# Fused key turning, fences on the carried part, and a new instruction order in a retention-plus-channel-mix kernel

## The chip, the cores and the metric

The kernel runs on one core of a Trainium2 chip, as one program. The metric is the device time of one execution in microseconds. TensorE (PE) multiplies, VectorE (DVE) and ScalarE (ACT) move and combine, GpSimd (POOL) and SyncE (SP) issue most of the transfers.

## The reference

Two layers follow each other. Batch 4, 8 heads, 768 tokens, head size 64; model size 512, inner size 1024.

```python
state = gamma * state + einsum('bhd,bhe->bhde', k[:, :, t], v[:, :, t])
y[:, :, t] = einsum('bhd,bhde->bhe', q[:, :, t], state) / sqrt(D)
...
x_prev = x shifted by one token
xk = mu_k * x + (1 - mu_k) * x_prev
xr = mu_r * x + (1 - mu_r) * x_prev
out = sigmoid(xr @ w_r) * (relu(xk @ w_k) ** 2 @ w_v)
```

Here x is y with the heads side by side.

## The kernel before

The work is cut into 12 blocks of 256 tokens, three to each batch entry, so blocks 0, 3, 6 and 9 begin a sequence. A block passes through retention and then through the channel mix.

Retention of block n, by the short names that the kernel gives its steps: `lq`, `lk`, `lv` load queries, keys and values (GpSimd's queue mostly). `vs` scales the values by the decay. `Tq` and `Tk` turn queries and keys on PE, `Eq` and `Ek` copy the turned blocks from PSUM on ACT. `S` multiplies turned keys by turned queries (scores, in two parts for blocks 0 to 5), and `M` masks them on DVE. `C` makes the products of keys and values that change the state; `U` adds them up (DVE, two sums in blocks 0 to 5 and four in the later ones); `G` decays the sum for the next block (ACT). The output is gathered in one pair of PSUM banks: `I` adds the part of the carried state whose input rows and output bank lie crosswise, `Y` the part inside the block, and `J` the rest of the carried part (in blocks 0, 1 and 6 to 11 `Y` includes it). `D` multiplies by the decay table `gy` on DVE and gives x.

Channel mix: `dx` is the difference of neighbouring tokens, `X.n.0.j` and `X.n.1.j` are the mixed inputs for w_k and w_r, four pieces each (DVE; for block 0 `t` prepares them on ACT). `K` multiplies by w_k, `Qa` and `Qb` take Relu and square on ACT, `R` and `s` make the gate, `V` multiplies by w_v, `O` combines on DVE, `st` stores. Blocks 3 and 4, 6 and 7, 9 and 10 share their mixed inputs and `K` in pairs.

Three sets of blocks differ in the tiles used. Blocks in `WHOLE` are turned with 128-row tiles: 16 matmuls of 128 rows and 64 columns. The others are turned in quarters of the array: 32 matmuls of 64 by 64. `HALF` (6 to 11) also does its scores, products and outputs in quarters of the array. `WIDE` (2 to 5) uses whole 128-row products.

The order of everything is written out by hand in the string `ORDER`: each word is one step, `~` names its engine and `@` the PSUM banks of a PE step. The loop at the end of the kernel calls the steps in that order, and each engine executes its own in that order. Waits between engines follow from the data. `z` steps multiply zeros, to keep PE busy while it would wait at the start.

Of the kernel before, what the change touches and what calls it, by code (L numbers as in the profile page):

```python
# [9 lines left out]
F16 = mybir.dt.float16  # L10
# [18 lines left out]
wk.1~p G.0~a z.2@6 Tq.1@6 Eq.1~a vs.1~p lq.2~p Tk.1@7 Ek.1~a M.0.0.0.2~v M.0.1.2.4~v Y.0 D.0~v
t.0.0.3~a t.0.0.2~a t.0.0.1~a lv.2~p z.2@4 S.1.1@23 M.1.1~v C.1@01 U.1.0~v z.2@4 I.1@23 S.1.0@67  # L30
X.0.0.1~v t.0.1.2~a X.0.0.2~v Tk.2@0 t.0.1.3~a t.0.0.0~a M.1.0~v X.0.0.0~v z.2@4 Y.1 t.0.1.1~a
X.0.0.3~v Ek.2~a K.0.0@0 K.0.1@6 lq.4~p U.1.1~v G.1~a wr~p lk.4~p D.1~v dx.1~v X.1.0.2~v X.1.0.0~v
K.0.2@1 Qa.0.0~a Qb.0.0~a Qa.0.2~a lq.3~p X.1.0.1~v X.1.0.3~v X.1.1.0~v Qa.0.1~a K.0.3@0 Qa.0.3~a
lk.3~p vs.2~v Tq.2@1 X.1.1.2~v K.1.3@6 K.1.0@0 C.2@7 U.2.0~v lv.3~p Eq.2~a S.2.1@23 M.2.1~v S.2.0@45
M.2.0~v Qb.0.3~a lv.4~p K.1.1@1 X.1.1.1~v Qa.1.0~a t.0.1.0~a K.1.2@7 I.2@23 Qb.0.1~a Qa.1.1~a wv.0~p
Qb.0.2~a Tq.4@01 Eq.4~a Y.2 Qa.1.3~a Qb.1.1~a X.0.1.3~v X.1.1.3~v R.1.1@4 Tk.4@01 Ek.4~a J.2 R.1.0@6
Qa.1.2~a s.1.0~a X.0.1.2~v X.0.1.1~v X.0.1.0~v R.0.1@5 s.0.1~a s.1.1~a R.0.0@7 s.0.0~a S.4.1@01
Qb.1.0~a D.2~v dx.2~v X.2.0.2~v X.2.0.0~v S.4.0@23 Tq.3@4 Eq.3~a X.2.0.1~v wv.1~p X.2.0.3~v Tk.3@7
lq.5~p Ek.3~a K.2.2@5 Qa.2.2~a K.2.3@4 M.4.1~v M.4.0~v Qa.2.3~a Qb.2.3~a lk.6~p S.3.1@67 M.3.1~v
S.3.0@01 vs.3~p C.3@23 U.3.0~a Qb.2.2~a K.2.1@4 Qa.2.1~a K.2.0@2 Qa.2.0~a I.3@45 lq.6~p vs.4~v  # L40
C.4@67 U.3.1~v X.2.1.1~v V.0.1.0@3 M.3.0~v V.1.0.0@2 G.3~a U.4.0~v I.4@01 X.2.1.3~v U.4.1~v J.3
Qb.1.3~a Y.4 Qb.2.0~a lk.5~p X.2.1.2~v X.2.1.0~v Y.3 D.3~v dx.3~v V.0.0.0@7 V.0.1.1 O.0.1~v Tq.5@45
J.4 D.4~v dx.4~v R.2.0@6 Qb.2.1~a V.0.0.1 O.0.0~v X.3.0.1~v Eq.5~a Qb.1.2~a V.1.0.1 X.3.0.2~v
O.1.0~v Tq.6@01 Eq.6~a Tk.6@45 Ek.6~a st.0.0~s lk.7~p st.1.0~s V.1.1.0@3 V.1.1.1 O.1.1~v s.2.0~a
R.2.1@0 s.2.1~a lv.5~p X.3.0.0~v X.3.0.3~v Tk.7@67 Ek.7~a G.4~a S.6@45 M.6~v Tk.5@23 Ek.5~a vs.5~v
V.2.0.0@0 K.3.2@1 Qa.3.2~a K.3.0@6 S.5.0@23 M.5.0~v S.5.1@45 C.5@1 U.5.0~v K.3.3@7 Qb.3.2~a Qa.3.0~a
lq.7~p K.3.7@6 Qa.3.3~a Qa.3.7~a lv.6~p lq.8~p vs.6~v M.5.1~v V.2.0.1 st.0.1~s I.5@67 O.2.0~v
st.2.0~s C.6@23 U.6.0~a U.6.1~v U.6.2~v K.3.6@1 Qa.3.6~a lk.9~p X.3.1.3~v Y.5 Tq.7@45 Eq.7~a U.6.3~v
X.3.1.2~v I.6@01 J.5 X.3.1.0~v D.5~v X.3.1.1~v Qb.3.3~a G.6~a V.2.1.0@2 K.3.1@3 V.2.1.1 O.2.1~v
Qb.3.7~a Qa.3.1~a Qb.3.1~a dx.5~v K.3.4@4 K.3.5@5 Qa.3.5~a X.5.0.0~v X.5.0.3~v R.3.1@2 s.3.1~a  # L50
lv.7~p Qa.3.4~a X.5.0.1~v Qb.3.4~a R.3.0@5 R.4.0@2 s.3.0~a s.4.0~a Qb.3.0~a X.5.0.2~v vs.7~v K.5.2@4
S.7@67 st.1.1~s M.7~v Qb.3.5~a Y.6 Qb.3.6~a lv.10~p C.7@23 U.7.0~v X.5.1.1~v Qa.5.2~a K.5.0@5
R.4.1@6 Qa.5.0~a D.6~v s.4.1~a V.4.0.0@4 V.4.0.1 V.3.1.0@5 U.7.1~v Qb.5.0~a X.5.1.3~v U.7.2~v I.7@01
X.5.1.2~v U.7.3~v Tq.8@67 Eq.8~a X.5.1.0~v O.4.0~v lv.8~p vs.8~v Qb.5.2~a lq.10~p lk.8~p Tk.8@23
Ek.8~a V.3.1.1 V.3.0.0@4 C.8@67 O.3.1~v st.2.1~s st.3.1~s Y.7 dx.6~v D.7~v Tq.10@23 V.3.0.1 Eq.10~a
G.7~a dx.7~v X.6.0.2~v V.4.1.0@5 R.5.1@2 s.5.1~a K.5.3@0 Qa.5.3~a R.5.0@2 U.8.0~v O.3.0~v V.4.1.1
lv.9~p lk.10~p lq.9~p Tk.10@01 s.5.0~a U.8.1~v X.6.0.1~v Ek.10~a X.6.0.0~v Tk.9@23 Ek.9~a K.5.1@7
Qa.5.1~a X.6.0.3~v K.6.0@4 lq.11~p Qb.5.1~a Qa.6.0~a U.8.2~v I.8@01 vs.9~v S.8@23 M.8~v O.4.1~v
# [26 lines left out]
def kernel(  # L85
# [126 lines left out]
    def first(n):  # L212
        return n % NB == 0
# [586 lines left out]
```

## Time and profile before

| | |
|---|---|
| times shown | 153.05, 240.62 (median), 286.7 us |
| span of the profiled execution | 151.4 us |
| around the span (153.05 less 151.4) | 1.65 us |
| granted TensorE clock | 1.00 |
| PE busy | 143.4 us, 95% |
| DVE busy | 127.8 us, 84% |
| ACT busy | 103.6 us, 68% |
| POOL busy | 55.3 us, 37% |
| transferred | 22.16 MB |

The profile is of one execution; its span belongs to the lowest of the three times. Busy time of an engine is the union of its instructions, so matmuls that overlap count once. An instruction's own duration contains its way through the pipeline; what a step costs in a dense stretch is the distance from its start to the next step's start.

### The profile page before, as it was taken

To read this page: it belongs to the slowest core of one execution; us is meant where nothing else is said; L and a number is where in the kernel's file an instruction comes from. 1 tells how busy PE (TensorE), PEld (TensorE's weight loads), DVE (VectorE), ACT (ScalarE), POOL (GpSimd) and SP (SyncE) were. 2 spreads that over 40 slices of the span, in tenths; PEclk is the share of its full clock that TensorE was granted. 3 is DMA by queue.
4 is the path that set the end of the run, shared out by engine and by line. 5 is a ranking of instruction groups with operands and counts; after the bars stand their busy time and mean duration, and the time that the engine had idled before them with its cause. 6 is when DMAs were issued, how large, how long until landed. Compare 5 with 4: busy or idle time off the path is not lost.

```text
span 151.4 us, 5541 instructions
## 1 busy us (share of the span) xinstructions
PE 143.4 (95%) x2426; PEld 82.8 (55%) x2426; DVE 127.8 (84%) x212; ACT 103.6 (68%) x195; POOL 55.3 (37%) x65
## 2 busy tenths in 40 slices
PE   7878799999999999999999999999999999999991
PEld 3345487757754554547465564548456444655450
DVE  7886999999989999999999999999799999400432
ACT  3565979899844795779567786999604756839420
POOL 7953998577957309996710000000000000000000
PEclk9999999999999999999999999999999999999999
DMA  5999999999999999999999019301000005500433
GB/s 140 219 229 197 207 231 192 168 251 212 196 167 202 233 262 107 256 300 198 231 173 126 7 38 283 105 35 45 0 4 0 4 0 211 205 0 0 148 133 139
DMA packets 45624, 22.16 MB, mean 146 GB/s; under 512 B 37400, under 2 KB 41248, under 8 KB 45600
## 3 DMA queue, kind: packets, MB, share of 16 engines
q0 software_dynamic: 38704, 14.42, 74.5%
q1 hardware_dynamic: 6592, 7.21, 14.3%
q8 instruction: 19, 0.31, 0.8%
q10 hardware_dynamic: 304, 0.18, 0.4%
q14 instruction: 5, 0.04, 0.1%
HBM read 24.16 MB, written 6.29 MB: 201 GB/s over the span
## 4 chain that ended last, share of the span: by engine, by line
PE 73%; DMA 12%; POOL 11%; issue 1%; DVE 0%; POOLq 0%
PE ps L624 27%; PE ps L572 14%; DMA v<-in_v_dram 12%; PE ps L612 12%; PE ps L582 8%; PE ps L278 3%; POOL q L235 3%; POOL k L230 2%; PE ps L441 2%; POOL vs L253 2%; POOL v L230 2%; PE ps L366 1%; PE ps L462 1%; PE ps L642 1%; PE ps L318 1%
## 5 line engine op out<-in xcount | busy, mean ns | idle before, releaser
L624 PE MATMUL ps<-wv,k2s 128*128 128x512 f16 x184 | 44.1, 380 | 0.0
L591 ACT ACTIVATE kr<-ps 128x512 f32<-128x512 f32 x48 | 27.9, 594 | 12.5 <-PE ps L582 6.5
L624 PEld LDWEIGHTS <-k2s 128*128 128x128 f16 x184 | 17.1, 98 | 18.9 <-ACT k2s L603 0.4
L630 DVE SCALAR_TENSOR_TENSOR os<-ps,rs 128x512 f32<-128x512 f32 x23 | 15.6, 684 | 11.9 <-ACT rs L618 9.4
L612 PE MATMUL ps<-wr,xr 128*128 128x512 f16 x96 | 23.5, 379 | 0.0
L582 PE MATMUL ps<-xk,wk 128*128 128x256 f16 x192 | 23.2, 273 | 0.0
L572 PE MATMUL ps<-xk,wk 128*128 128x512 f16 x96 | 23.0, 379 | 0.0
L618 ACT ACTIVATE rs<-ps 128x512 f32<-128x512 f32 x24 | 13.6, 597 | 12.9 <-PE ps L612 12.1
L230 POOL DMA_DIRECT2D k<-in_k_dram x20 | 17.8, 903 | 10.3 <-PE ps L384 6.7
L582 PEld LDWEIGHTS <-wk 128*128 128x128 f16 x192 | 18.1, 98 | 3.7
L241 ACT COPY qT<-ps 128x1024 f16<-128x1024 f16 (+1 forms) x13 | 12.3, 946 | 9.5 <-PE ps L278 7.8
L558 DVE SCALAR_TENSOR_TENSOR xr<-dx,mu,xT 128x256 f16<-128x256 f32 (+1 forms) x32 | 17.9, 577 | 0.1
L230 POOL DMA_DIRECT2D v<-in_v_dram x18 | 16.0, 911 | 3.6 <-DMA wr<-in_moe_w_r_dram 1.9
L558 DVE SCALAR_TENSOR_TENSOR xk<-dx,mu,xT 128x256 f16<-128x256 f32 (+1 forms) x32 | 17.0, 579 | 0.2
L354 DVE TENSOR_TENSOR a<-ps,c_sb 128x1024 f16<-128x1024 f32 (+1 forms) x14 | 14.6, 1066 | 0.9 <-PE ps L339 0.6
L603 ACT ACTIVATE k2s<-kr 128x512 f16<-128x512 f32 x24 | 14.8, 631 | 0.3
L612 PEld LDWEIGHTS <-xr 128*128 128x128 f16 x96 | 9.0, 97 | 10.7 <-issue 0.5
L572 PEld LDWEIGHTS <-wk 128*128 128x128 f16 x96 | 9.1, 98 | 10.5
L599 ACT ACTIVATE k2s<-kr 128x512 f16<-128x512 f32 x24 | 14.5, 627 | 0.3
L241 ACT COPY kT<-ps 128x1024 f16<-128x1024 f16 (+1 forms) x13 | 12.2, 945 | 2.2 <-PE ps L272 1.7
L529 DVE TENSOR_TENSOR dx<-xT 128x1024 f32<-128x1024 f32 x11 | 13.4, 1221 | 0.2
L253 DVE TENSOR_TENSOR vs<-v,csm_sb 128x1024 f16<-128x1024 f32 x10 | 12.2, 1217 | 0.2 <-DMA v<-in_v_dram 0.2
(73 smaller groups left out, 165.6 us busy)
## 6 DMA issues: line engine op xcount, KB each, us to landing
out_dram<-os SPq DMA_DIRECT2D x23, 256.0 KB, 2.4
v<-in_v_dram POOLq DMA_DIRECT2D x18, 256.0 KB, 7.7
q<-in_q_dram POOLq DMA_DIRECT2D x11, 256.0 KB, 8.4
k<-in_k_dram POOLq DMA_DIRECT2D x21, 128.0 KB, 8.8
v<-in_v_dram POOLq DMA_DIRECT2D x2, 512.0 KB, 7.2
wk<-in_moe_w_k_dram POOLq DMA_DIRECT2D x2, 512.0 KB, 10.4
wv<-in_moe_w_v_dram POOLq DMA_DIRECT2D x2, 512.0 KB, 10.4
wr<-in_moe_w_r_dram POOLq DMA_DIRECT2D x1, 512.0 KB, 8.7
```

The costliest lines, as they stand in the source:

```text
L230: e.dma_start(out=dst[:, :, i * D : i * D + D], in_=src[:, i * P : i * P + P].rearrange("h p d -> p h d"),)
L241: e.copy(out=out, in_=in_)
L253: e.tensor_tensor(out=VS(n), in0=V32(n).rearrange("p h (i d) -> p i h d", i=2), in1=gks[:, int(half(n) or wide(n)), :, :, None].to_broadca ...
L354: nc.vector.tensor_tensor(out=a_full(n)[:, i, :, j0:j1], in0=pairs(banks("S", n, i, j0))[:, :, j0:j1], in1=(below if wide(n) else causal[: ...
L558: nc.vector.scalar_tensor_tensor(out=XM[w](k)[:, j, t0:t1], in0=DX(k)[:, j, t0:t1], scalar=mu[:, w * NCO + j : w * NCO + j + 1], in1=x[:, ...
L572: nc.tensor.matmul(banks("K", n, g), lhsT=wk16[:, co, g * P : g * P + P], rhs=XM[0](k)[:, co, :], start=(co == 0), stop=(co == NCO - 1),)
L582: nc.tensor.matmul(pz[:, i, :], lhsT=wk16[:, co, fo * P : fo * P + P], rhs=XM[0](k)[:, co, m * TM + t0 : m * TM + t1], start=(i == 0 and c ...
L591: nc.scalar.activation(out=kr, in_=banks("K", n, g, *u), func=AF.Relu)
L603: nc.scalar.activation(out=K2(n)[:, w * g : w * g + w, t0:t1], in_=kr.rearrange("p a t -> p (a t)").rearrange("p (i t) -> p i t", i=w), fu ...
L612: nc.tensor.matmul(banks("R", n, tb), lhsT=XM[1](k)[:, co, t : t + P], rhs=wr16[:, co, :], start=(co == 0), stop=(co == NCO - 1),)
L624: nc.tensor.matmul(banks("V", n, tb), lhsT=K2(n)[:, fo, tb * P : tb * P + P], rhs=wv16[:, fo, :], start=(fo == 0), stop=(fo == NFO - 1),)
L630: nc.vector.scalar_tensor_tensor(out=OS(2 * n + tb), in0=banks("V", n, tb), scalar=1.0 / (KSC * KSC), in1=RS(2 * n + tb), op0=ALU.mult, op ...
```

## The change

Five things change.

1. Blocks 4 and 5 are added to `WHOLE`, so their queries and keys are turned by 16 matmuls of 128 rows.
2. In blocks 6 to 11 (`MERGED`) `Tk` and `C` fall away. A new step `TC` multiplies each block of K by two things side by side, a 64 by 64 identity and the scaled values, 128 columns in one pass. It has two parts, `TC.n.0` and `TC.n.1`, of 16 matmuls each. The identity stands ahead of the values in the same buffer, which therefore has a ninth group of 64 columns and is filled by three new small steps on DVE. `Ec` copies the turned part, now in 32-bit PSUM, in two halves of 512 on ACT in place of one copy of 1024.
3. A new step `w` stands behind each `I`: ACT copies a few elements of the bank pair into a small buffer. What is accumulated there next waits for that copy.
4. The weights w_k come in three parts (quarter, half, quarter) in place of two halves, and the values of block 11 move from SyncE's queue to GpSimd's. The scaling of block 3's values moves from GpSimd to DVE.
5. The string `ORDER` is another one.

```diff
-WHOLE = (0, 1, 2, 3)
+WHOLE = (0, 1, 2, 3, 4, 5)
 WIDE = (2, 3, 4, 5)
+MERGED = (6, 7, 8, 9, 10, 11)
...
-    VS = ring("vs_", 3, [2, H, D], F16)
+    VI = ring("vs_", 3, [2 * H + 1, D], F16)
...
+    def VS(n):
+        return VI(n)[:, 1:].rearrange("p (i h) d -> p i h d", i=2)
...
+    fenced = const.tile([P, 2, NJ, 2], F32, name="fenced")
...
+    def both(n, i):
+        return banks("TC", n, i).rearrange("p u (j x t) -> p u j x t", j=NJ, x=2)
+
+    def turned_state(e, n, i):
+        ps = both(n, i)
+        for j in range(NJ):
+            for u in range(2):
+                for a, h, jo, hp in heads(j):
+                    k = 1 + i * H + h
+                    x = slice(0, 2) if more(n) or not (u and i) else slice(0, 1)
+                    nc.tensor.matmul(
+                        ps[low(a), u, j, x], lhsT=K16(n)[low(u), h, i * D : i * D + D],
+                        rhs=VI(n)[low(u), 0 : k + 1 : k][:, x],
+                        start=(j == 0), stop=(j == NJ - 1), skip_group_check=True,
+                    )
+
+    def turned_k_part(e, n, i):
+        copy(
+            e, KT(n)[:, :, i].rearrange("c j (u p) -> c u j p", u=2), both(n, i)[:, :, :, 0],
+        )
...
+        if merged(n):
+            src = both(n, c // 2)[:, c % 2, :, 1]
...
+    def fence(e, n):
+        us = slice(0 if half(n) or not first(n) else 1, 2)
+        e.copy(out=fenced[:, us], in_=pairs(banks("I", n))[:, us, :, 0:C:W])
...
-            ((step, 2, ALU.is_ge), (below, 0, ALU.is_ge)),
+            ((step, 2, ALU.is_ge), (below, 0, ALU.is_ge))
+            + tuple((VI(i)[:, 0], 2, ALU.is_equal) for i in range(3) if MERGED),
...
-    def load_wk(e, h):
-        f = slice(h * dff // 2, (h + 1) * dff // 2)
+    def load_wk(e, a, b):
+        f = slice(a * dff // 4, b * dff // 4)
```

Of the new `ORDER`, one piece before and the piece that stands for it now:

```diff
-D.2~v dx.2~v X.2.0.2~v X.2.0.0~v S.4.0@23 Tq.3@4 Eq.3~a X.2.0.1~v wv.1~p X.2.0.3~v Tk.3@7
+D.2~v K.1.0@1 U.3.1~v dx.2~v S.4.1@67 Qa.1.0~a G.3~a S.3.0@45 M.3.0~v X.2.0.1~v Qb.1.0~a
```

The first place is DVE from the output of block 2 (`xT0<-ps`) on. In the names, `xk_2` is the mixed input for `K` of block 2, `a2` the masked scores, `vs` the scaled values, `t32` and `tg2` the state sums. Before:

```order
L514 TENSOR_TENSOR xT0_130<-ps_61,gy_sb_122 128x2x4x128
L529 TENSOR_TENSOR dx_0_99<-xT0_130 128x4x256
L558 SCALAR_TENSOR_TENSOR xk_2_103<-dx_0_99,mu_125,xT0_130 128x256 x4
L354 TENSOR_TENSOR a2_1_84<-ps_61,c16_sb_120 128x1024 x2
L354 TENSOR_TENSOR a2_0_83<-ps_61,c16_sb_120 128x1024
L253 TENSOR_TENSOR vs_1_75<-v32_0_70,csm_sb_121 128x1024
```

and with the change:

```order
L547 TENSOR_TENSOR xT0_130<-ps_61,gy_sb_122 128x2x4x128
L452 TENSOR_TENSOR t32_0_86<-ps_61,tg2_0_93 128x256
L566 TENSOR_TENSOR dx_0_99<-xT0_130 128x4x256
L364 TENSOR_TENSOR a2_0_83<-ps_61,c16_sb_120 128x1024
L595 SCALAR_TENSOR_TENSOR xk_2_103<-dx_0_99,mu_125,xT0_130 128x256
L364 TENSOR_TENSOR a2_0_83<-ps_61,c16_sb_120 128x1024
L263 TENSOR_TENSOR vs_1_75<-v32_0_70,csm_sb_121 128x1024
L364 TENSOR_TENSOR a2_1_84<-ps_61,c16_sb_120 128x1024
L452 TENSOR_TENSOR tg2_1_94<-ps_61,tg0_1_88 128x256
L595 SCALAR_TENSOR_TENSOR xk_2_103<-dx_0_99,mu_125,xT0_130 128x256 x2
L452 TENSOR_TENSOR t32_0_86<-ps_61,tg2_1_94 128x256
L595 SCALAR_TENSOR_TENSOR xk_2_103<-dx_0_99,mu_125,xT0_130 128x256
```

The masks of blocks 3 and 4, the scaling of block 4's values and the state sums, which stood behind the four mixed inputs of block 2, stand between them now.

The second place is ACT, where block 6 begins (`qT_77` and `kT_80` are its turned queries and keys). Before:

```order
L241 COPY qT_77<-ps 128x2x4x128
L241 COPY kT_80<-ps 128x2x8x64
L618 ACTIVATE rs_112<-ps 128x512
L618 ACTIVATE rs_113<-ps 128x512
L241 COPY kT_81<-ps 128x2x8x64
```

and with the change, where `fenced` is the new small copy:

```order
L251 CAST tg_0_90<-ps 128x256
L251 COPY qT_77<-ps 128x2x4x128
L555 COPY fenced<-ps 128x16
L251 CAST kT_80<-ps 128x2x4x64
L628 ACTIVATE kr_107<-ps 128x512
L628 ACTIVATE kr_110<-ps 128x512
L636 ACTIVATE k2s<-kr_107 128x2x256
L251 CAST kT_80<-ps 128x2x4x64
```

One copy of the turned keys has become two, with other work between them, and the fence of block 5 stands ahead of the first.

The third place is GpSimd's queue around the values of block 3 (`v_3_73`). Before:

```order
L738 DMA wr_129<-in_moe_w_r_dram 128x4x512
L230 DMA k_0_66<-in_k_dram 128x8x64 x2
L235 DMA q_3_65<-in_q_dram 128x8x128
L230 DMA k_3_69<-in_k_dram 128x8x64 x2
L230 DMA v_3_73<-in_v_dram 128x8x64 x2
```

and with the change:

```order
L245 DMA q_3_65<-in_q_dram 128x8x128
L245 DMA q_0_62<-in_q_dram 128x8x128
L240 DMA v_3_73<-in_v_dram 128x8x64 x2
L240 DMA k_3_69<-in_k_dram 128x8x64 x2
L773 DMA wk_127<-in_moe_w_k_dram 128x4x256
L776 DMA wr_129<-in_moe_w_r_dram 128x4x512
```

The values of block 3 are issued ahead of the keys of block 3 and of the gate weights w_r, and the last quarter of w_k comes behind them.

More of the change, by code (lines that the diff above doesn't have):

```diff
@@ L29 @@
[L29 to L34, printed above, removed]
@@ L81 @@
+Vc.11.1.0@2 Oc.11.1.0~v sc.11.1.0~s
 """
```

127 lines of the change are left out of this document (68 added, 59 removed).

## The prediction

> **What bounds the kernel now.** I read the page first, then the busy times by stretch, then the end of the chain that ended last, then the timeline around the first blocks.
>
> ```profile
> PE 143.4 (95%) x2426; PEld 82.8 (55%) x2426; DVE 127.8 (84%) x212; ACT 103.6 (68%) x195; POOL 55.3 (37%) x65
> ...
> PE   7878799999999999999999999999999999999991
> ...
> DVE  7886999999989999999999999999799999400432
> ...
> POOL 7953998577957309996710000000000000000000
> ```
>
> TensorE (PE) is at nine tenths or more from the sixth slice to the last but one; VectorE (DVE) is as full, but stops ten slices before the end.
>
> ```profile
> core 0: us, PE busy (x) PEld busy (x) DVE busy (x) ACT busy (x) POOL busy (x), PEclk, DMA share, GB/s
> 0.00:10.00 10.00, 7.77 (x90) 3.87 (x90) 8.29 (x31) 4.78 (x10) 8.62 (x14) 1.00 1.10 178
> 10.00:20.00 10.00, 7.76 (x230) 5.24 (x230) 8.11 (x14) 7.13 (x16) 6.34 (x7) 1.00 1.51 220
> 20.00:30.00 10.00, 9.92 (x160) 7.92 (x158) 9.82 (x16) 8.88 (x18) 7.72 (x9) 1.00 1.67 196
> 30.00:38.00 8.00, 7.67 (x140) 5.07 (x140) 7.93 (x12) 7.94 (x14) 6.26 (x8) 1.00 1.30 229
> 38.00:50.00 12.00, 12.00 (x230) 7.08 (x230) 11.51 (x16) 7.05 (x15) 9.16 (x11) 1.00 1.90 192
> 50.00:60.00 10.00, 10.00 (x197) 5.13 (x195) 9.81 (x13) 8.07 (x15) 3.33 (x5) 1.00 1.13 204
> ...
> 120.00:130.00 10.00, 10.00 (x49) 4.50 (x46) 9.82 (x19) 6.89 (x14) 0.00 (x0) 1.00 0.29 110
> 130.00:140.00 10.00, 10.00 (x64) 6.08 (x62) 0.59 (x2) 7.05 (x15) 0.00 (x0) 1.00 0.12 47
> ```
>
> From 38 us PE has no gap at all, and DVE hardly any until 130. So two engines are full at once: PE sets the end, and DVE, which makes almost everything that PE multiplies, is only just ahead. ScalarE (ACT) is not full anywhere.
>
> ```profile
> 147.37 0.89 PE ps L642 x8
> 148.26 0.02 issue
> 148.28 0.42 DVE os L649
> ```
>
> The chain ends with the last matmul at 148.26; the span is 151.4, so 3.15 us follow it (multiply, store, landing). A microsecond that PE waits anywhere after its first feed-forward matmul therefore comes out at the end, and one that PE is spared comes off, as long as DVE keeps ahead.
>
> The sum is made against this execution: 151.4 us of span and 1.65 around it, 153.05, the lowest of the three times shown. Their median, 240.62, is 57% above it; no row of the page accounts for that, and I forecast the time of an execution like the profiled one.
>
> **The change: VectorE's order before block 2.** This is the term that decides. The first feed-forward matmul of block 2 (step K.2) needs its four mixed inputs X.2.0 from DVE.
>
> ```profile
> 13.95 1.23 DVE L514 TENSOR_TENSOR xT<-ps,gy_sb 128x1024 f32<-128x1024 f32 x1 [1.19 <-PE ps L441]
> ...
> 19.47 3.67 PE L582 MATMUL ps<-xk,wk 128*128 128x256 f16 x32
> ...
> 33.58 1.67 DVE L558 SCALAR_TENSOR_TENSOR xk<-dx,mu,xT 128x256 f16<-128x256 f32 x4
> ...
> 35.12 1.92 PE L582 MATMUL ps<-xk,wk 128*128 128x256 f16 x16
> 35.17 3.54 DVE L354 TENSOR_TENSOR a<-ps,c_sb 128x1024 f16<-128x1024 f32 x3
> ...
> 35.98 1.90 POOL L253 TENSOR_TENSOR vs<-v,csm_sb 128x1024 f16<-128x1024 f32 x1 [0.53 <-DMA v<-in_v_dram]
> ...
> 38.63 1.22 DVE L253 TENSOR_TENSOR vs<-v,csm_sb 128x1024 f16<-128x1024 f32 x1
> 39.76 0.42 DVE L419 TENSOR_TENSOR t<-ps,tg 128x256 f32<-128x256 f32 x1
> 40.09 0.48 DVE L558 SCALAR_TENSOR_TENSOR xr<-dx,mu,xT 128x256 f16<-128x256 f32 x1
> ```
>
> Before, from the output multiply of block 0 (13.95) to the end of X.2.0 (33.58 + 1.67 = 35.25) DVE works 21.3 us with hardly a gap. In the new order the same stretch holds the same instructions and nine more: the masks of blocks 3 and 4 (four, 3.54/3 = 1.18 each), the scaling of the values of blocks 3 and 4 (two; start to start 39.76 - 38.63 = 1.13 each; that of block 3 ran on GpSimd until now, 1.90 there), and three state sums (0.33 apart). Together 4.72 + 2.26 + 1.0 = 8.0 us. The stretch may begin a little sooner: DVE waited 1.19 us at 13.95, and the new order puts the last piece of the decay table there; against that it has three more small masks. Bounds -0.7 and +0.5; I take -0.3, nearer the gain, since that table piece has to be done anyway. So X.2.0 ends at 13.95 - 0.3 + 21.3 + 8.0 = 42.95, and K.2 can start at 42.8, where it was 35.12.
>
> **What PE has until then.** Its feed-forward work starts at about 19.6 now (both masks of block 1 stand ahead of the last X.0.0: 13.65, and 1.23 + 2 x 1.18 + 0.33 + 5 x 0.4 of DVE work) against 19.47.
>
> ```profile
> 28.33 0.42 PE L278 MATMUL ps<-c_sb,q 64*64 64x64 f16 x32
> ...
> 34.11 0.64 PE L272 MATMUL ps<-c_sb,q 128*64 128x128 f16 x16
> ...
> 34.58 0.61 PE L272 MATMUL ps<-c_sb,k 128*64 128x128 f16 x16
> ...
> 36.98 0.62 PE L331 MATMUL ps<-qT,kT 64*128 64x128 f16 x16
> ...
> 37.93 0.44 PE L384 MATMUL ps<-vs,k 128*64 128x64 f16 x16 [0.33 <-POOL vs L253]
> ...
> 40.16 0.30 PE L441 MATMUL ps<-qT,tg 64*64 64x128 f16 x4
> ...
> 42.59 0.42 PE L441 MATMUL ps<-qT,tg 64*64 64x128 f16 x12
> ...
> 42.94 1.08 PE L478 MATMUL ps<-a,vs 128*64 128x128 f16 x32
> ```
>
> Before, PE passed from 19.47 to 35.12 in 15.65 us. Added ahead of K.2 are, with the overlap at each end taken off: the turning of block 2's keys (0.57), two scores of block 3 (1.15), states of blocks 3 and 4 (0.74), their carried parts (0.8), their inner parts (1.02), both turnings of block 5 (1.1), and the dearer turning of block 4 (two steps of 16 passes at 0.6 in place of two of 32 at 0.42: some 0.2 to 0.4). That is 5.6, so PE is through at 19.6 + 15.65 + 5.6 = 40.85 and waits about 1.95 us for DVE. It cannot skip ahead: behind K.2 in its queue stand the rest of K.2 and the value matmuls of blocks 0 and 1, which were ready long before.
>
> **What remains after K.2.** Before, 148.26 - 35.12 = 113.1 us. Off go the steps now done ahead (1.15 + 0.74 + 0.8 + 1.02 and the old turnings of block 5, 0.64: 4.35) and the wait for GpSimd's scaling that the 37.93 row shows (0.4 with its weight load). Left: 108.35.
>
> **One pass of K for blocks 6 to 11.** Six times, 32 short passes that turn K and 32 (24 in blocks 8 and 11) that make the state become 32 passes of twice the width, in two steps.
>
> ```profile
> 18.79 0.64 PE L489 MATMUL ps<-a,vs 64*64 64x128 f16 x32 [0.28 <-DVE a L354]
> ...
> 52.38 0.38 PE ps L278 x32
> 52.75 0.26 PE ps L318 x32
> ```
>
> The nearest row to the new form (same tile, 128 wide) takes 0.64 for 32, 0.84 if each half pays its own 0.2 of run-out; the two old steps take 0.26 to 0.38 each inside the dense stretch. Gain per block between +0.1 (a loss) and -0.2; in all +0.6 to -1.2, I take -0.3, since the page's rows in dense flow lie close together. The TensorE stretches of short steps that interrupt full-width matmuls also fall from 25 to 23, which is inside that bound. [...]
>
> **The fences and ScalarE.**
>
> ```profile
> L241 ACT COPY kT<-ps 128x1024 f16<-128x1024 f16 x11 | 11.0, 1010 | 0.5 <-PE ps L278 0.5
> ...
> L441 PE MATMUL ps<-qT,tg 64*64 64x64 f16 x176 | 3.7, 197 | 0.0
> ...
> L241 ACT COPY kT<-ps 128x512 f16<-128x512 f16 x2 | 1.2, 586 | 1.7 <-PE ps L272 1.7
> ...
> L694 ACT COPY mu<-ps 128x8 f32<-128x8 f32 x1 | 0.2, 183 | 0.0
> ```
>
> Twelve tiny copies of 0.18 us are 2.2 us, and two copies of 0.59 for one of 1.01 add 0.17 six times: ACT goes from 103.6 to 107 of 151, covered by its own idle time. What can cost is the wait: the next accumulating step on that bank now waits for the carried part to run out (0.2), the copy (0.18) and two signals, about 0.5 in all, plus whatever ACT is busy with. Zero where other PE work lies between, which it does for nine of twelve; the whole 0.5 at most at blocks 2, 9 and 4. Block 2's falls into time that PE has to wait for DVE anyway. I take 0.3, bounds 0 and 6 (twelve times 0.5). Behind a waiting fence on ACT stand Relus and turned copies, on which PE waits only later.
>
> DMA edits: the weights of K in three parts and the values of block 11 in GpSimd's queue (two issues of 0.9) cost nothing, since GpSimd is idle after 76 us; the values of block 3 are issued ahead of the last quarter of those weights and are needed by DVE only at about 31 us.
>
> After K.2 both engines run in step again: the next things PE needs of DVE (the scaling of blocks 5 and 6) stand at nearly the same distance on both. Each small DVE gap there (0.7 us before, from 38 to 60) can now reach PE; I add 0.6, bounds 0 and 2.
>
> **Sum.** 42.8 + 108.35 - 0.3 + 0.3 + 0.6 = 151.75 for the last matmul, + 3.15 + 1.65 = 156.55; I say **156.5 us**, 2.3% slower. A measurement of this kernel can tell about 2% (3 us) from no change.
>
> **Rivals.** *The fences decide.* If half of the twelve cost 0.5 because ACT is in the middle of something, 3 us come on top: 159.5. For it: ACT is 7 to 9 tenths busy from 20 us on. Against: most have other matmuls between. *The wait for DVE does not come*, because masks and scaling turn out to be spread otherwise or the start is sooner: then PE goes on at 40.85 and the end is 40.85 + 108.35 + 3.15 + 1.65 = 154.0, less 0.3: 153.7, no change. Against: DVE has 0.25 us of gap in 20 to 38 us. [...]
>
> **How the numbers follow.** Forecast 0.52 (its own spread is 154.5 to 158.5, of which 0.40 lies above 156.1, the 2% line, and 0.12 below), fences 0.22, no wait 0.12, passes by number 0.14 (0.08 of it without the wait, faster). Slower 0.40 + 0.22 = 0.62, the same 0.12 + 0.12 + 0.06 = 0.30, faster 0.08. The range that leaves out the fast case and the far end of the fences is 152.5 to 160.5.
>
> **What would show it.** In the new profile: K.2's first matmul near 43 us with a PE wait on DVE just before it, the last X.2.0 ending within 0.5 us of that; PE without gaps over 0.5 us afterwards; the scaling of block 3 on DVE at about 31; the fused step of 32 passes at 0.6 to 0.85 us; the fences at 0.2 us each. The forecast is wrong if K.2 starts before 41, if PE shows several waits on the small copies, or if the last matmul ends before 149.

## The result and the profile after

The changed kernel takes **159.17 us** in the median of four executions (157.82 to 159.84), against 153.05 and 153.69 of before; the ratio is **1.037, with an interval of 1.030 to 1.044**. The forecast was 156.5, with 152.5 to 160.5 as its range. (Two more executions of before took 240.62 and 286.7 us; no row of a page accounts for them, and they are left out. In the later sessions before took 153.2 to 153.4 in the median.) Ratios compare the faster executions of a kernel with the faster ones of before. The direction and the range held, the size did not: 2.7 us more than forecast.

The profiled execution of after has a span of 158.1 us. Four lines of its page, in the same columns as before:

```profile
PE 148.8 (94%) x2194; PEld 83.7 (53%) x2194; DVE 129.3 (82%) x216; ACT 104.5 (66%) x213; POOL 56.0 (35%) x67
...
PE   7999998799999999967999999999999999999991
...
DVE  6989999999999999649988999999799699310532
...
PEclk9999999999999999997899999999999999999999
```

PE is still the full engine. But it has a dent that was not there before, in the 18th and 19th slice, just behind one in DVE, and in the 19th and 20th slice its granted clock is down. The busy times by stretch show the same place, in the columns used for before:

```profile
core 0: us, PE busy (x) PEld busy (x) DVE busy (x) ACT busy (x) POOL busy (x), PEclk, DMA share, GB/s
...
20.00:30.00 10.00, 8.46 (x146) 6.41 (x144) 9.93 (x17) 7.44 (x13) 8.54 (x11) 1.00 1.68 211
30.00:38.00 8.00, 7.55 (x126) 5.06 (x125) 7.94 (x10) 7.94 (x18) 5.86 (x8) 1.00 1.55 212
...
60.00:70.00 10.00, 9.45 (x115) 4.25 (x113) 6.29 (x11) 9.46 (x20) 6.56 (x9) 1.00 1.23 266
70.00:80.00 10.00, 8.28 (x105) 4.30 (x106) 9.76 (x16) 3.92 (x7) 7.77 (x10) 0.83 1.52 224
```

From 20 to 38 us PE is idle for 2 us, where before it was idle for 0.4 in the same two stretches. From 60 to 70 DVE is idle for 3.7 us, and right behind that PE loses 1.7 us and its clock. PE's waits, by what ended them (total, times, longest):

```profile
PE ps L282 <- DMA q<-in_q_dram: 1.5, 2, 1.2
PE ps L423 <- DVE vs L263: 1.4, 1, 1.4
...
PE ps L495 <- DVE a L357: 0.6, 1, 0.6
PE ps L474 <- ACT fenced L555: 0.3, 1, 0.3
```

**The place ahead of block 2.** Rows of the timelines of DVE and PE:

```profile
30.12 1.22 DVE L263 TENSOR_TENSOR vs<-v,csm_sb 128x1024 f16<-128x1024 f32 x1
...
41.65 0.48 DVE L595 SCALAR_TENSOR_TENSOR xk<-dx,mu,xT 128x256 f16<-128x256 f32 x1
```

```profile
28.12 0.64 PE L282 MATMUL ps<-c_sb,q 128*64 128x128 f16 x16 [1.20 <-DMA q<-in_q_dram]
...
42.29 0.31 PE L474 MATMUL ps<-qT,tg 64*64 64x128 f16 x8
42.53 1.92 PE L619 MATMUL ps<-xk,wk 128*128 128x256 f16 x16
```

The last mixed input of block 2 is done at 42.13 and K.2 starts at 42.53, without a gap before it. PE has already lost its 2 us: 1.55 on late queries, and 0.27 and 0.18 on a fence and on another copy of ACT.

**The place that was not foreseen.** GpSimd, DVE and PE around 70 us, a group of rows for each engine's timeline:

```profile
56.59 1.75 POOL L245 DMA_DIRECT2D q<-in_q_dram  x2 [6.70 <-PE ps L423]
58.32 5.31 POOL L240 DMA_DIRECT2D v<-in_v_dram  x6
```

```profile
69.53 1.23 DVE L263 TENSOR_TENSOR vs<-v,csm_sb 128x1024 f16<-128x1024 f32 x1 [3.68 <-DMA v<-in_v_dram]
```

```profile
70.91 0.42 PE L423 MATMUL ps<-vs,k 64*64 64x128 f16 x16 [1.40 <-DVE vs L263]
71.94 0.45 PE L495 MATMUL ps<-a,vs 64*64 64x64 f16 x32 [0.62 <-DVE a L357]
...
72.94 3.32 PE L649 MATMUL ps<-wr,xr 128*128 128x512 f16 x8 [0.20 <-DVE os L667]
76.05 1.33 PE L661 MATMUL ps<-wv,k2s 128*128 128x512 f16 x4
```

GpSimd's queue stands still for 6.70 us with the load of block 10's queries at its head, which waits until PE has read what lies in its buffer. The queries of block 9 and then the values of block 7 stand behind it. The values are issued from 58.32 on and land 9.9 to 10.2 us after their issue; DVE has been idle for 3.68 us by then, and PE waits 1.40, then 0.62 for the mask that DVE makes next, then 0.20. After that the eight gate matmuls take 76.05 - 72.94 = 3.11 us, 389 ns each, where they take 215 elsewhere: the granted clock is 0.50 for 3.4 us, from 73.2 to 76.6.

The standing still alone is not new. In before, GpSimd's queue and DVE show this at the same place:

```profile
57.11 1.75 POOL L230 DMA_DIRECT2D k<-in_k_dram  x2 [6.67 <-PE ps L384]
58.84 5.30 POOL L230 DMA_DIRECT2D v<-in_v_dram  x6
```

```profile
69.25 1.22 DVE L253 TENSOR_TENSOR vs<-v,csm_sb 128x1024 f16<-128x1024 f32 x1
```

There the keys of block 9 stand at the head, the values of block 7 are the first two of the six issues behind them, and they go out even later. But they land 4.9 to 5.1 us after their issue, behind 256 KB of keys in place of 512 KB of queries, and DVE comes to scale them only at 69.25. With the change it is ready for them at 65.85. So two things meet: the values land some 5 us later, and they are wanted 3.4 us sooner. As early as they landed in before, they would have been in time for 65.85.

The end, in the chain that ended last, is as before: 0.42 of DVE behind the last matmul, and the store.

```profile
154.00 0.89 PE ps L679 x8
154.89 0.02 issue
154.91 0.42 DVE os L686
```

### The profile page after: what moved, and what is told of

It reads as the page before. It is cut to its first block, busy times and chain, and to the rows that moved or that the text cites. A ratio compares the mean times of both kernels' runs of the same rounds, so it can differ in the third digit from the quotient of the medians.

```text
span 158.1 us, 5129 instructions
## 1 busy us (share of the span) xinstructions
PE 148.8 (94%) x2194; PEld 83.7 (53%) x2194; DVE 129.3 (82%) x216; ACT 104.5 (66%) x213; POOL 56.0 (35%) x67
## 4 chain that ended last, share of the span: by engine, by line
PE 68%; DMA 16%; POOL 8%; issue 3%; DVE 2%; ACT 1%; DVEq 0%; POOLq 0%
PE ps L661 23%; PE ps L649 13%; DMA v<-in_v_dram 11%; PE ps L619 10%; PE ps L609 10%; DMA q<-in_q_dram 5%; POOL q L245 3%; PE ps L474 2%; PE ps L423 1%; POOL v L240 1%; PE ps L282 1%; PE ps L495 1%; PE ps L679 1%; POOL k L240 1%; POOL k L245 1%
## 5 line engine op out<-in xcount | busy, mean ns | idle before, releaser
L661 PE MATMUL ps<-wv,k2s 128*128 128x512 f16 x184 | 44.8, 381 | 0.0
L661 PEld LDWEIGHTS <-k2s 128*128 128x128 f16 x184 | 17.6, 99 | 19.5 <-issue 1.1
L649 PE MATMUL ps<-wr,xr 128*128 128x512 f16 x96 | 25.4, 397 | 0.2 <-DVE os L667 0.2
L619 PE MATMUL ps<-xk,wk 128*128 128x256 f16 x192 | 24.5, 273 | 0.0
L609 PE MATMUL ps<-xk,wk 128*128 128x512 f16 x96 | 23.8, 379 | 0.1
L240 POOL DMA_DIRECT2D v<-in_v_dram x20 | 17.9, 911 | 6.8 <-DMA wr<-in_moe_w_r_dram 1.9
L595 DVE SCALAR_TENSOR_TENSOR xk<-dx,mu,xT 128x256 f16<-128x256 f32 (+1 forms) x32 | 17.5, 579 | 0.1
L263 DVE TENSOR_TENSOR vs<-v,csm_sb 128x1024 f16<-128x1024 f32 x11 | 13.3, 1219 | 3.7 <-DMA v<-in_v_dram 3.7
L649 PEld LDWEIGHTS <-xr 128*128 128x128 f16 x96 | 9.5, 100 | 11.4 <-issue 2.0
L245 POOL DMA_DIRECT2D q<-in_q_dram x12 | 10.6, 893 | 8.3 <-PE ps L423 6.7
```

Of the source, the lines that this page charges most:

```text
L240: e.dma_start(out=dst[:, :, i * D : i * D + D], in_=src[:, i * P : i * P + P].rearrange("h p d -> p h d"),)
L245: e.dma_start(out=dst, in_=src.rearrange("h (p i) d -> p h (i d)", i=2))
L595: nc.vector.scalar_tensor_tensor(out=XM[w](k)[:, j, t0:t1], in0=DX(k)[:, j, t0:t1], scalar=mu[:, w * NCO + j : w * NCO + j + 1], in1=x[:, ...
L609: nc.tensor.matmul(banks("K", n, g), lhsT=wk16[:, co, g * P : g * P + P], rhs=XM[0](k)[:, co, :], start=(co == 0), stop=(co == NCO - 1),)
L619: nc.tensor.matmul(pz[:, i, :], lhsT=wk16[:, co, fo * P : fo * P + P], rhs=XM[0](k)[:, co, m * TM + t0 : m * TM + t1], start=(i == 0 and c ...
L649: nc.tensor.matmul(banks("R", n, tb), lhsT=XM[1](k)[:, co, t : t + P], rhs=wr16[:, co, :], start=(co == 0), stop=(co == NCO - 1),)
```

## The experiments

Source lines shift by a few between kernels, so the same step has other L-numbers. "Word" is a word of the string `ORDER`. The theory at the start: the 2.7 us above the forecast are the late values of block 7, the clock that falls after them, and nothing else. The rival: the waits there are made up for later, or other steps are dearer than assumed.

**1. The values of block 7 ahead of the queries of block 10.**

```diff
-lq.10~p R.2.1@2 X.3.1.2~v s.2.1~a K.3.4@3 lq.9~p Qa.3.4~a Qb.3.4~a Qa.3.2~a lv.7~p lv.9~p
+lv.7~p lq.10~p R.2.1@2 X.3.1.2~v s.2.1~a K.3.4@3 lq.9~p Qa.3.4~a Qb.3.4~a Qa.3.2~a lv.9~p
```

> The changed kernel with one issue moved: in GpSimd's queue the values of block 7 stand ahead of the queries of block 10. Theory (values of block 7 arrive late because the issue for block 10 blocks the queue until block 6's queries are turned, PE then waits about 2.2 us between 68 and 73 us, and its clock falls for 3 us, 1.7 us more): no wait of DVE on those values, no clock below 1.00, span 154.0 to 154.8, time 155.6 to 156.4. Rival (fences and the tight DVE order set the pace, the wait only shows there): under 1 us less than the changed kernel, the waits reappear at the next fused step.

Measured: 156.78 us, ratio 1.024 (1.022 to 1.026), clock 1.00. Two rows of GpSimd's timeline, and one of PE's:

```profile
50.28 1.77 POOL L240 DMA_DIRECT2D v<-in_v_dram  x2 [0.19 <-issue]
56.49 1.77 POOL L245 DMA_DIRECT2D q<-in_q_dram  x2 [4.44 <-PE ps L423]
```

```profile
71.98 1.24 PE L649 MATMUL ps<-wr,xr 128*128 128x512 f16 x5 [0.83 <-issue]
```

The queries still wait, 4.44 us now, but the values have gone out ahead of them, and DVE scales them without a wait. One moved word takes off 2.4 us, and what is left is within 0.3 of the forecast of 156.5. It did not get below 156.4, since a new stop of 0.83 us stands in the same place, released by nothing that the profile shows; experiment 10 returns to it.

**2. Work for the wait.** Multiplications of zeros (`z.6@7`, four matmuls that take 1.4 us) ahead of the first fused step of block 7, in after.

> The changed kernel with 1.3 us of zero matmuls put ahead of the first fused step of block 7, into PE's wait for the values. Theory (the clock falls because PE is idle for 2.2 us within 5): the wait stays, the granted clock stays at 1.00, R of block 4 takes 1.75 us and not 3.1; about 1.5 us less than executions whose clock fell, the same as those where it did not (156.0 to 157.0 of span). Rival (the clock falls for another reason): clock 0.989 and 158 us as before.

Measured: 158.77 us, 1.037 (1.035 to 1.040). The clock stays at 1.00 through 68 to 80 us. But PE then stops for 1.30 us in the middle of the short passes:

```profile
70.77 0.42 PE L423 MATMUL ps<-vs,k 64*64 64x128 f16 x16
...
73.33 0.21 PE L423 MATMUL ps<-vs,k 64*64 64x128 f16 x1 [1.30 <-issue]
```

With the zeros the clock stayed up in all four executions (0.997 to 0.999), where it fell in two of after's four. The time is that of after all the same: 158.58 to 159.21, against 157.82 and 158.74 of after without the fall and 159.60 and 159.84 with it. Filling the wait saved nothing here, since the new stop came in its place.

**3. The queries of blocks 2 and 4 earlier** in GpSimd's queue, ahead of its scaling of block 1 and of the keys of block 4.

```diff
-lk.2~p vs.1~p ... D.1~v lq.2~p Tq.2@1 ... lk.4~p ... Ek.4~a lq.4~p
+lk.2~p lq.2~p vs.1~p ... D.1~v Tq.2@1 ... lq.4~p lk.4~p ... Ek.4~a
```

> The changed kernel with the queries of block 2 issued ahead of GpSimd's scaling of block 1 and those of block 4 ahead of the keys of block 4. Theory A (DVE's order before block 2 is the limit, only 0.4 us behind the late queries): PE's two waits on queries (0.35 and 1.2 us) go, but the first matmul of K for block 2 moves only from 42.5 to 42.0 to 42.2; time 0.3 to 0.6 us less. Theory B (the queries alone were the limit): it moves to 41.0, time 1.5 us less.

Measured: 158.52 and 158.53 us, and 161.28 and 161.48 where the granted clock was 0.989; 1.035 (1.033 to 1.037). PE's waits for the queries are gone, and K.2 starts later, not sooner, which neither theory had:

```profile
26.49 1.23 DVE L263 TENSOR_TENSOR vs<-v,csm_sb 128x1024 f16<-128x1024 f32 x1 [0.83 <-DMA v<-in_v_dram]
...
42.66 0.47 DVE L595 SCALAR_TENSOR_TENSOR xk<-dx,mu,xT 128x256 f16<-128x256 f32 x1
```

```profile
43.32 1.92 PE L619 MATMUL ps<-xk,wk 128*128 128x256 f16 x16
```

The values of block 2 came later in exchange, DVE lost 0.83, the last mixed input moved by 1.0, and K.2 followed it by 0.8. That speaks for DVE as what sets K.2: PE had the queries in time and won nothing, it waited for masks and scaled values of DVE instead (0.62 and 0.22).

**4. The fences in the order of before.** The new code with the old `ORDER`, `WHOLE` up to block 3 and no `MERGED`, and each fence word right ahead of the step that must wait for it. (Block 3's inner part goes ahead of the rest of its carried part, as in the changed kernel, and one run of zeros is split over two banks.)

> The kernel before with the twelve small ACT copies added, each ahead of the step that goes on accumulating in that bank (the inner part of block 3 is moved ahead of its remaining carried part, and a third of the first zero matmuls goes to another bank). Theory (a fence costs only where PE has nothing between, 0.5 us at most): PE waits on the copies 1 to 2 us in all, since this order was not made for them; 0.5 to 1.5 us slower than before. Rival (the fences decide the slowdown): 4 us or more slower.

Measured: 163.62 us, 1.068 (1.065 to 1.071). The rival held. Two of PE's eight waits:

```profile
15.32 0.63 PE L521 MATMUL ps<-a,vs 64*64 64x128 f16 x30 [1.47 <-ACT fenced L554]
...
34.06 0.31 PE L473 MATMUL ps<-qT,tg 64*64 64x128 f16 x8 [1.20 <-ACT fenced L554]
```

A fence of 0.17 us costs 1.2 to 1.5 where a copy or two of ACT stand ahead of it in ACT's queue. The eight waits together are 7.6 us; 1.2 more are a wait of K.2 for mixed inputs, of the kind that experiment 6 shows.

**5. The same fences, each directly behind its carried part** (`I.n@.. w.n~a`).

> The order of before with the twelve fences, each issued to ScalarE right behind its carried part instead of right ahead of the inner part (163.62 us there, TensorE waiting 7.6 us in eight places for fences). Theory (the place in ScalarE's queue is what costs): the waits on fences fall below 2.5 us in all, 156.5 to 159 us. Rival (the fence costs as such, by its copy, two signals and the run-out, about 0.8 us each time): 161 to 164, TensorE still waiting over 5 us for them.

Measured: 156.67 us, 1.023 (1.020 to 1.026). No wait on a fence is left. Most of the rest hangs on one place:

```profile
29.05 0.17 ACT L553 COPY fenced<-ps 128x16 f32<-128x16 f32 x1 [2.07 <-PE ps L472]
```

```profile
30.29 0.44 PE L286 MATMUL ps<-c_sb,q 64*64 64x64 f16 x30 [1.27 <-ACT kr L626]
...
38.40 1.98 PE L617 MATMUL ps<-xk,wk 128*128 128x256 f16 x15 [1.17 <-DVE xk L593]
```

Here the fence of block 2 stands too early: ACT idles 2.07 us for the carried part, with Relus behind it that PE is waiting for. The 1.17 us in K.2 have another part to them: the four mixed inputs take 3.36 us in this kernel, where they took 1.67, beside GpSimd's scaling. Experiment 6 comes to that.

**6. That one fence three steps of ACT later** (`I.2@23 Qb.0.1~a Qa.1.1~a wv.0~p Qb.0.2~a w.2~a`).

> The order of before with the twelve fences, each right behind its carried part in ScalarE's queue, but that of block 2 three Relus and squares later, right ahead of the copy of block 4's queries. Where it stood, ScalarE idled 2.07 us with four of those behind it, and TensorE waited 1.27 for a Relu and 1.17 for the mixed inputs. Theory (that one place is the whole loss of 3.4 us, the fences cost nothing by themselves): 153.0 to 154.2 us, no wait of TensorE on a fence, K.2 at 35 to 36. Rival (the eleven others cost 0.2 to 0.3 each): 155.5 to 156.7.

Measured: 1.005 (1.002 to 1.009). The median is 154.82, but the twelve executions lie in two groups, six at 153.55 to 154.07 and six at 155.56 to 157.75, and the profiled one belongs to the second. In it:

```profile
34.70 3.44 DVE L593 SCALAR_TENSOR_TENSOR xk<-dx,mu,xT 128x256 f16<-128x256 f32 x4
```

```profile
35.93 1.91 POOL L261 TENSOR_TENSOR vs<-v,csm_sb 128x1024 f16<-128x1024 f32 x1
```

Four mixed inputs take 3.44 us where they took 1.67 before: 1.8 us more, nearly the 1.9 in which GpSimd scales the values of block 3. Before, that scaling began at 35.98, when the mixed inputs were done. No execution of the faster group has a profile; that this place is what parts the two groups is the reading that experiment 7 puts to the test.

**7. Block 3's values scaled on DVE in that kernel** (`X.2.0.3~v vs.3~v` in place of `vs.3~p`).

> The order of before with the twelve fences well placed, and besides the scaling of block 3's values on VectorE, right behind the mixed inputs of block 2, in place of GpSimd. In the profile without this, GpSimd's scaling (35.93, 1.91 us) lay over the mixed inputs X.2.0 on VectorE, which took 3.44 us in place of 1.67, and K.2 waited 1.45; the executions lay at 153.6 to 154.1 or at 155.6 to 157.8. Theory (an instruction of VectorE with two inputs in SBUF cannot run beside GpSimd's): X.2.0 takes 1.7 us, K.2 waits under 0.3, and the executions lie in one group at 153.0 to 154.0. Rival (VectorE is full, and the 1.2 us that it takes over come out at the end): 154.5 to 156. Rival (the second group has another cause): still two groups, 2 us apart.

Measured: 155.12 us (154.69 to 155.35, one group), 1.011 (1.009 to 1.013). The theory has its mixed inputs and its one group, and the rival that DVE is full has the time; the theory's 153 to 154 is missed:

```profile
34.38 1.67 DVE L593 SCALAR_TENSOR_TENSOR xk<-dx,mu,xT 128x256 f16<-128x256 f32 x4
```

```profile
35.92 1.92 PE L617 MATMUL ps<-xk,wk 128*128 128x256 f16 x16
...
39.50 0.44 PE L392 MATMUL ps<-vs,k 128*64 128x64 f16 x16 [0.73 <-DVE a L362]
```

The mixed inputs are back at 1.67, K.2 does not wait, and there is one group. But DVE is full, and the 1.2 us it took over come out as waits of 0.20 and 0.73 on PE soon after, 1.4 us at the end against the lower group. The change moves the same scaling to DVE.

**8. Masks ahead of the mixed inputs.** The kernel of 6, with `M.4.1~v` ahead of `X.2.0.2~v` and `M.4.0~v` ahead of `X.2.0.1~v`.

> The same as the first of these, with the two masks of block 4 ahead of the mixed inputs of block 2 on VectorE, as the change has them; nothing else is moved. Theory (each instruction put ahead of X.2.0 on VectorE costs its own time at the end): K.2 starts 2.2 to 2.9 us later with a wait of TensorE on the mixed inputs, and the end is 2.0 to 2.9 later, 155.2 to 157. Rival (TensorE makes it up, since the masks are done when they are next wanted): under 0.8 us more.

Measured: 159.60 us, 1.041 (1.038 to 1.044), dearer than the theory had it.

```profile
37.92 0.27 PE L617 MATMUL ps<-xk,wk 128*128 128x256 f16 x1 [1.92 <-DVE xk L593]
39.45 2.84 PE L617 MATMUL ps<-xk,wk 128*128 128x256 f16 x15 [1.26 <-DVE xk L593]
```

PE waits 3.2 us for the mixed inputs. GpSimd's scaling lies over them here too, and 1.45 of these stood in the profiled execution of 6 without the masks, so the two masks add 1.7. Then the 15 passes take 2.77 us to the next step instead of 1.65: the clock fell again. From the scores ahead of K.2 to the last matmul PE takes 153.99 - 34.37 = 119.62 us, where it took 151.08 - 34.68 = 116.40 in 6. That is 3.2 more: the added wait and the fall of the clock (0.50 for 3.4 us), with next to nothing made up.

**9. Mixed inputs ahead of masks, in the kernel of 1.** X.2.0 goes ahead of the masks of block 3, the second of block 4 and the scaling of block 4, and K.2's first two steps ahead of the inner parts of blocks 3 and 4.

```diff
-M.3.0~v X.2.0.1~v ... M.3.1~v ... vs.4~v ... M.4.1~v ... X.2.0.3~v ... X.2.0.0~v U.4.1~v G.4~a X.2.0.2~v K.2.1@2
+X.2.0.1~v X.2.0.3~v X.2.0.0~v X.2.0.2~v M.3.0~v ... M.3.1~v ... vs.4~v ... K.2.1@0 M.4.1~v ...
```

> The change with the values of block 7 issued ahead of the queries of block 10 (156.78 us by itself), and besides, on VectorE, the four mixed inputs of block 2 (X.2.0) ahead of the masks of block 3, the second mask of block 4 and the scaling of block 4; on TensorE the first two steps of K.2 ahead of the inner parts of blocks 3 and 4. Theory (VectorE's order ahead of block 2 costs the other 3 us or most of it): X.2.0 ends near 36.9 instead of 42.1, K.2 starts at 39.3 to 39.9 instead of 42.4 and some of the work that stood ahead of it follows; TensorE loses 1.3 to 2.0 us less, 154.8 to 155.5 us. Rival (TensorE's own steps there have grown, the order of VectorE does not matter): 156.4 to 157.1. Rival (the masks that are now later make TensorE wait as long behind K.2): 156.4 or more, with waits on a in 39 to 45.

Measured: 161.09 us, 1.053 (1.049 to 1.057). The third reading held, and it cost more than it said: K.2 starts at 40.75, but a gate step ahead of it waits 1.61 us for the bank that a mask has not yet emptied, and waits of 0.56 and 0.87 follow behind it.

```profile
37.84 2.75 PE L649 MATMUL ps<-wr,xr 128*128 128x512 f16 x12 [1.61 <-DVE a L364]
```

PE needs the masks as well as the mixed inputs there. My reordering of DVE only moved the wait.

**10. Fused or not.** The kernel of 1 with blocks 6 to 11 turned and multiplied separately, `Tk` where `TC.n.0` stood (or the first of the two) and `C` in place of the second.

> The change with the values of block 7 ahead of the queries of block 10 (156.78), and besides blocks 6 to 11 as before: K turned by 32 short passes where the first fused step stands, the state made by 32 or 24 where the second stands, one copy of 1024 columns in place of two of 512. Theory (a short pass costs 8 to 10 ns in four quarters, the fused one 19): 156.3 to 157.5. [...]

Measured: 160.77 and 161.90 us, and 163.51 and 163.79 where the granted clock was 0.989; 1.053 (1.047 to 1.058). So it is 4.0 to 5.1 us dearer than with the fusing, and well above the 156.3 to 157.5 of the theory. But the passes themselves are a small part of that:

```profile
81.52 0.70 PE L287 MATMUL ps<-c_sb,k 64*64 64x64 f16 x56
84.29 0.26 PE L287 MATMUL ps<-c_sb,k 64*64 64x64 f16 x8 [2.07 <-issue]
```

56 short passes start within 0.7 us, some 12 ns each; then PE stops for 2.07 us in the middle of a step, and for 1.13 in another place. The profiled executions differ by 161.90 - 156.55 = 5.35 us. 2.4 of them are such stops (3.2 here, 0.83 in the kernel of 1) and 1.1 is a new wait for a mixed input. The passes themselves are 0.7: the 192 fused ones take 3.6 us from start to start, the 368 separate ones 4.3 here and 3.9 in before. The other 1.1 are smaller pieces that were not followed up.

The two stops come at the 1119th and the 1375th matmul, 256 apart. The stops in experiments 1 and 2 come at the 1118th (a record more or less can be missing), in a gate step in 1 and, with four matmuls more ahead of it, in a fused step in 2: the number stays, the step does not. One row of the page counts what the instruction queue moved, 18 packets and 0.29 MB in this kernel, so 16 KB each:

```profile
q8 instruction: 18, 0.29, 0.8%
```

In the records of the single transfers, a packet of that queue begins at 82.10 in this kernel and takes 0.95 us; PE goes on 1.24 after it. In experiment 2 it begins at 70.54, takes 1.33, and PE goes on 1.46 after it. The traces of all experiments have ten such stops, of 0.5 to 2.2 us, and at each PE goes on 1.2 to 1.5 us after a packet has ended. That reads as PE having run out of instructions. The pages count 2370 matmuls to the 18 packets here, 2426 to 19 in before and 2194 to 17 in the kernel of 1: 128 to 132 to a packet, which agrees with the spacing. No stop belongs to 16 of the 17 packets in the kernel of 1 and to 16 of the 18 here; the others cost 0.8 to 2.1 us each.

**11. 128-row tiles for blocks 4 and 5, in the orders of 4 and of 6.**

```diff
-WHOLE = (0, 1, 2, 3)
+WHOLE = (0, 1, 2, 3, 4, 5)
-Tq.4@01 ... Tk.4@01 ... Tq.5@45 ... Tk.5@23
+Tq.4@0 ... Tk.4@1 ... Tq.5@4 ... Tk.5@2
```

> The order of before with the twelve fences right ahead of the inner parts (163.62 us), and besides queries and keys of blocks 4 and 5 turned by 128-row tiles (16 passes each in place of 32). Theory: each of the four turnings takes 0.15 to 0.25 us more on TensorE, 0.6 to 1.0 in all, 164.2 to 164.7. Rival (half as many passes cost less): 162 to 163.3.

> The same, and besides queries and keys of blocks 4 and 5 turned by 128-row tiles (16 passes each in place of 32). Theory: 0.6 to 1.0 us more than without, four times 0.15 to 0.25 of TensorE. Rival (hidden or cheaper): within 0.3 of it.

Measured: 165.53 us (1.081, 1.076 to 1.087), 1.9 above the kernel of 4, and 162.85 (1.060, 1.057 to 1.064), 8 to 9 above that of 6. The turnings themselves, start to start, take 0.57 in place of 0.27, so 1.2 for all four. The profiled executions in the order of 6 differ by 161.87 - 155.95 = 5.9 us, and the rest of that is again stops without a releaser, 4.7 us in three places, two of them here (in four of the six executions behind the median of 162.85 the granted clock was 0.989 or 0.990, in the profiled one 1.00):

```profile
82.26 0.32 PE L286 MATMUL ps<-c_sb,q 64*64 64x64 f16 x16 [1.14 <-issue]
...
87.63 0.45 PE L286 MATMUL ps<-c_sb,q 64*64 64x64 f16 x32 [2.19 <-issue]
```

**12. The same, with the old count of instructions.** Sixteen more short passes ahead of each of the four turnings, into a place that the turning then overwrites.

```diff
+            if n in (4, 5):
+                for j in range(j0, j1):
+                    for i in range(2):
+                        for s, h, jo, hp in heads(j):
+                            nc.tensor.transpose(
+                                pt[low(s), j, i, 0:64], src[low(0), h, i * D : i * D + D],
+                                ident[low(0), low(0)],
+                            )
```

> The order of before with well placed fences and blocks 4 and 5 turned by 128-row tiles (162.85 us; TensorE stops there three times, 4.7 us in all, released by nothing that the profile shows, at the 863rd, 1247th and 1375th matmul: multiples of 128 apart), and besides, ahead of each of these four turnings, 16 more short passes into the same bank (their results are overwritten), so that every later instruction of TensorE has the number again that it has in the kernel without the 128-row tiles (153.6 in its fast runs), which has no such stop. Theory (the stops are TensorE waiting for the next 16 KB of its instructions, and come where a stretch of short passes ends at such a border): the stops are gone or under 1 us in all, 155 to 157 us, the added passes themselves taking 0.3 us four times. Rival (the stops come from the banks that the new turnings use, or from later copies): they stay, 161 to 164.

Measured: 157.63 us (157.34 to 157.93), 1.029 (1.026 to 1.032). With 64 matmuls **more**, the kernel is 5.2 us faster, and all three stops are gone. At the two places shown:

```profile
80.26 0.45 PE L294 MATMUL ps<-c_sb,q 64*64 64x64 f16 x32
...
83.41 0.47 PE L294 MATMUL ps<-c_sb,q 64*64 64x64 f16 x31
```

So the stops hang on which matmuls stand at a border of 128, not on the banks or the data. Why PE stops at one border and not at the next is left open. The time is 0.6 above the top of what was expected, and that is in the open part: this kernel's K.2 waits 1.35 us for mixed inputs beside GpSimd, as in 6.

## Why the prediction was right and wrong

**What bounds the kernel: right.** PE is at 94% and the last matmul, at 154.89, sets the end.

**VectorE's order ahead of block 2: right in size, wrong in what shows it.** Forecast: X.2.0 done at 42.95, K.2 at 42.8, PE losing 1.95 us. Measured: 42.13, 42.53 and 2 us. The nine more instructions on DVE are there, block 3's scaling at 30.1. But the wait does not stand right before K.2, as I said it would; the late queries take it earlier. That their sum is 2 us again is luck. Experiment 3 speaks for DVE as the limit behind them, and 7 and 8 show the price in the order of before: 1.4 us at the end for one instruction of 1.2 us, and for two masks 1.7 us of added waits, which are not made up, besides the clock.

**What remains after K.2: this is the step that failed.** Forecast 108.35 - 0.3 + 0.3 + 0.6 = 108.95, measured 154.89 - 42.53 = 112.36. That is 3.4 us more, and the waits of 1.40, 0.62 and 0.20 for the values of block 7, with the 1.7 of the clock behind them, are 3.9. The sentence that let them through is "DMA edits ... cost nothing, since GpSimd is idle after 76 us". It looked at the edits that the change names, and at the end of the queue. The new order also moved loads within GpSimd's queue, so that two loads of queries go out right ahead of these values, and it brought DVE to their scaling at 65.85 in place of 69.25. I had the row in which the queue stands still for 6.67 us in before, with the same values behind it, and did not follow which loads stand there in the new order and when DVE wants them. The 0.6 with its upper bound of 2 stood for small gaps of DVE, not for this. Experiment 1 shows that the late values are the cause; it moves them ahead of the standing still and of both loads of queries at once, so how much each of these does is not shown.

With that one word moved, the kernel ends at 156.78, and K.2 to the last matmul takes 151.60 - 42.40 = 109.20. That this comes so near to 108.95, and 156.78 to 156.5, is in part luck: it holds the stop of 0.83, which no term had, and none of the waits for fences and for DVE that the 0.3 and the 0.6 stood for.

**The clock: not in the forecast.** About 1.7 us of the 3.9 in the profiled execution are the halved clock; two of after's four executions show it, and two, at 157.82 and 158.74, do not.

**One pass of K: right for the passes, blind to what else they do.** -0.3 us for all six blocks is what the distances between starts show, 3.6 us against 3.9 in before. The chance of 0.14 for passes that cost by their number stands on a price per pass that no run shows: in experiment 10, 56 of them start within 0.7 us, 12 ns each, and all 368 take 4.3 us, 0.7 more than the 192 fused ones. That fewer passes would count by way of the instruction supply was in no rival, and in experiment 10 it is worth 2.4 us. In the profile of before none of these stops occurs, though no kernel here has more matmuls; so the saving is one of where the borders fall.

**The fences: right for this kernel, but the bound was too low.** Forecast 0.3, one wait of 0.27 measured, 0.17 us of ACT each. The upper bound of 6 us took 0.5 for each of twelve; with the words put where they read most naturally, the loss is 10 us (experiment 4), 7.6 of it direct. The bound should have counted what stands ahead in ACT's queue. Well placed, they cost about half a per cent in the order of before (6). So the rival in which the fences decide, 159.5, came nearest to the time, but its mechanism is not what the trace shows.

**The 128-row tiles: mis-sized.** 0.2 to 0.4 for block 4 and 0.46 for block 5 in the sum; measured 0.3 four times, 1.2.

**Where the change's loss lies**, then: about 2.4 us in the late values of block 7 with their clock (taken back by 1), and 3.5 us that remain in the kernel of 1. From its first matmul of K (19.33) to its last matmul PE takes 132.27 us there, and 128.79 in before. 2.0 of the 3.5 are idle time (2.46 in place of 0.43): 1.6 ahead of K.2 and the stop of 0.83. The other 1.5 lie in steps that follow each other without a gap. The 128-row tiles (1.2 in the orders of 4 and 6) and the fused passes (-0.3) are among them, but in this order they were not measured apart. Sizes of single parts in other orders are not strictly additive, and 6 to 8 were run in the order of before. What the kernel would take without any fence was not tried with the new code. No version here beats the kernel of before; the closest, 6, is 0.5% slower.

## What to carry to other kernels

When a new order is read, read every queue in it, the loads too: a transfer that waited for its buffer held up all transfers behind it (6.70 us in after), and the values of block 7 landed 9.9 to 10.2 us after their issue there, behind 512 KB, and 4.9 to 5.1 in before, behind 256 KB; the urgent one must stand in front. A sync step of 0.17 us cost up to 1.5 where it stood behind two copies (experiment 4), and held its engine for 2 where it stood ahead of work that others wanted (5); place it by the queue it runs in. Where PE runs many short passes, count instructions: a stop of 1 to 2 us that nothing releases, at matmuls that are multiples of 128 apart, as at the 1119th and the 1375th in 10, points to the instruction supply, and it moved with the count (12).

## What the hardware showed that I had not expected

- PE stopped for 0.5 to 2.2 us at matmuls whose numbers differ by multiples of 128, and went on 1.2 to 1.5 us after a 16 KB packet of the instruction queue had ended (experiment 10: the 1119th and the 1375th, 18 packets of 0.29 MB in all). Adding 64 short passes removed 4.7 us of it (12).
- In after the clock halved behind 2.2 us of idle time in three pieces (1.40, 0.62, 0.20) within some 3.4 us, and stayed at 0.50 for 3.4 us. In the order of 6 with 128-row tiles, 2.19 us in one piece left it at 1.00 in the profiled execution, while four of that kernel's six executions show a lower clock; in 8, 3.2 in two pieces brought it down. The same idle time does not always tell, and why is not shown.
- DVE's mixed inputs, with both inputs in SBUF, hardly advanced while GpSimd scaled: 3.44 us in place of 1.67, with 1.9 of GpSimd's work in between (experiment 6). Three masks of DVE, which read PSUM, did not grow beside it: 3.54 us in before with the same scaling over them, 3.48 in 7 without it.
